# Third batch's first stage moved behind the second batch's last rows, two thirds of its stores put off, and the conditions at the end nested

## The chip, the cores and the metric

The kernel runs on one core of one Trainium2 chip. Its engines are TensorE (PE, matmuls), VectorE (DVE), ScalarE (ACT), GpSimd (POOL) and the queue engine SyncE (SP). ACT, POOL and SP also issue DMAs, each in the order of its own program. The metric is the device time of one execution in microseconds, the median of several runs.

## What is computed

```python
X = np.fft.rfft(x, axis=1)                     # x: (8, 2496, 256) float32
y = np.fft.irfft(X * F[None], n=2496, axis=1)  # F: one complex filter, 1249 x 256
...
x = y.reshape(8 * 2496, 256)                   # 19968 tokens
expert_idx = token_ids * 2654435761 % 8
out[mask_e] = np.maximum(x[mask_e] @ w1[e], 0) @ w2[e]     # w1[e]: 256 x 1024, w2[e]: 1024 x 256
```

A filter in the frequency domain is applied along each of 8 sequences (batches), and then each token goes through the one of 8 experts that its number picks.

## The kernel before, in words

**The filter.** The transform of length 2496 is split as 39 x 64. A batch (class `Batch`) passes three stages, all in float32.
- Stage 1 (`stage1(u)`, u = 0 to 5): matmuls `pa` (line 226, the last at 220) on rows of x, copied by ACT (line 228 or 223) into a tile `t1` on the chip. Each pair of u makes a part v = 0, 1, 2, which is stored to a table `d1` in DRAM at line 252: parts 0 and 1 have 960 KB, part 2 has 600 KB and 40 KB. ACT issues these stores for batch 2 and POOL for the later ones. `t1` has two places, which parts use in turn.
- Stage 2 (`stage2(u)`, u = 0 to 10): `load2(g)`, g = 0 to 4, brings two times 256 KB of `d1` back in another layout (line 258, on SP); `forward(u)` makes matmuls `pb` (line 267) and multiplies with the filter on DVE (lines 273 to 277); `back(u-1)` makes matmuls `pc` (line 289), copied by ACT. After every second one POOL stores two times 256 KB to a table `d2` (line 296).
- Stage 3 (`stage3(u)`, u = 0 to 5): `load4(v)` brings part v of `d2` back (`t<-d`, line 366, on SP), matmuls `pd` (line 226, the last at 220) make rows of tokens, ACT (batches 0 and 1) or DVE copies them to a tile `o`, and POOL writes each row of 117 tokens to its places in a DRAM table `xs`, sorted by expert, with an indirect DMA (`scatter`, line 385; four for each u, two for the last).

Batches 0 and 1 keep their middle tables on the chip; for them `turn4(u)` (matmuls `pu`, line 354) goes ahead of each `stage3(u)`.

**The experts.** `xs` is read in tiles of 128 tokens, of which 159 always exist and up to 163 may. `step(i)` handles tile i: `load(i + 4)` loads rows of a pair of tiles (`xg<-xs`, line 756, four loads of 64 KB), `numbers(i)` copies token numbers on POOL (line 773), `up(i)` makes 32 matmuls `ups` (line 790; relu at 794 on ACT and 796 on DVE), `down(i)` makes 16 matmuls `dps` (line 802), and POOL scatters the result to the output (line 806). `weights(i + 2, 0)` and `weights(i + 2, 1)` on SP load an expert's 1 MB of w1 (line 416) and of w2 (line 419) where the tile's expert differs. `turn(i + 1)` on DVE (line 780) prepares the next tile.

**The order.** It is written by hand. `todo` holds pairs of a time and a piece of work, sorted by time. Pieces with a time under 0 are emitted ahead of the tiles. For a time of 0 or more the whole part is the tile, and a fraction under .5 places the piece ahead of `up(i)`, one of .5 or more between `up(i)` and `down(i)` ("first slot" and "second slot" below). Times are no microseconds. Each engine works through its instructions in the order in which they were emitted; an instruction that waits holds up all behind it on its engine, DMA issues among them. `part1`, `part2` and `part3` list the times of a batch's stages 1, 2 and 3 and of their loads; `begin()` opens the tiles' buffers and issues `load(0)` to `load(3)`, half of them on ACT, the others on SP. The first tiles hold tokens of batches 0 and 1 alone, so `load(0)` waits for the last scatter of batch 1.

Before the change the pieces ahead of the tiles end as follows (t4 is `turn4`, s1 to s3 the stages, L1, L2 the loads of stages 1 and 2; batch, then index):

```
t4(1,0) s3(1,0) t4(1,1) s1(2,0) s3(1,1) t4(1,2) s1(2,1) s3(1,2) s1(2,2) t4(1,3) s1(2,3) s3(1,3) t4(1,4) s1(2,4) s3(1,4)
t4(1,5) s1(2,5) s3(1,5) L2(2,0) begin L2(2,1) L2(2,2) L2(2,3) L1(3,0) L1(3,1) s2(2,0)
```

**The end.** Tiles 159 to 162 stand in three blocks, each under its own condition `tc.If(used > first tile of the block)` at line 843, one after the other. With these inputs there are 159 tiles, and no block is entered.

Of the kernel before, what the change touches and what calls it, by code (L numbers as in the profile page):

```python
# [36 lines left out]
NU = (HN + XG) // XG  # L37
# [6 lines left out]
NT = (N + E * (TB - 1)) // TB  # L44
# [8 lines left out]
NSURE = NT - 4  # L53
# [66 lines left out]
def kernel(  # L120
# [10 lines left out]
    nc = tc.nc  # L131
# [45 lines left out]
    def slot(kind):  # L177
        slots[kind].append(slots[kind].pop(0))
        return slots[kind][-1]

    class Batch:


# [55 lines left out]
        def stage1(self, u):  # L239
            if self.d1 is None:  # L240
                self.d1 = dpool.tile([N2, 2 * NS, C], F32, name=f"d1_{self.b}", tag="d1")
            v, half = divmod(u, XL // XG)
            sl = slice(half * XG, half * XG + XG)
            if half == 0:
                self.t1 = slot("t1")
            self.products(wf_t, (NR, NR), 2 * NS, self.x[v][:, sl, :], self.t1[:, sl, :], nc.scalar.copy, u, "pa")
            if half == 1:


                eng = nc.scalar if self.b == 2 else nc.gpsimd  # L250
                for dram, chip in self.parts(self.d1, self.t1, v):
                    eng.dma_start(out=dram, in_=chip)

        def load2(self, g):
# [137 lines left out]
    batches = [Batch(b) for b in range(B)]  # L392
# [5 lines left out]
    def weights(i, which):  # L398

        if i >= NT:  # L400
            return
        if i >= 2 and which == 0:
            ws[i] = ws[i - 2][0:2]
        eng, kw = nc.sync, {}
        if which == 0:
            ws[i].append(eng.value_load(chunk_i[0:1, 0, i:i + 1], min_val=0, max_val=E - 1))
            if i >= 2:
                ws[i].append(eng.value_load(chunk_i[0:1, 1, i:i + 1], min_val=0, max_val=1))
        e = ws[i][2]
        if i >= 2:  # L410
            kw = {"cond": ws[i][3]}
        if which == 0:


            for f in (slice(0, F // 2), slice(F // 2, F)) if i < 2 else (slice(0, F),):
                eng.dma_start(out=ws[i][0][:, :, f],
                              in_=moe_w1[bass.ds(e, 1)].rearrange("one (p dp) f -> p (one dp) f", p=P)[:, :, f], **kw)
        else:
            eng.dma_start(out=ws[i][1], in_=moe_w2[bass.ds(e, 1)].rearrange("one (fp p) d -> p (one fp) d", p=P), **kw)
# [19 lines left out]
    def load_tables(part):  # L439
        if part < 2:  # L440

            nc.gpsimd.tensor_copy(junk[:], first.x[2 * part][0:1, 0, 0:1])
        sl = S_PARTS[part]
        nc.sync.dma_start(out=d_t[:, sl, :], in_=d_dram.ap()[:, sl, :])
        for k in range(2):
            load_filter(k, sl)
# [207 lines left out]
    def spaced(t0, t1, n):  # L654
        return [t0 + (t1 - t0) * u / n for u in range(n)]

    def part1(b, at, loads=None):
        bt = batches[b]
        if loads is None:

            loads = [at[2 * v] - 2.5 * (at[1] - at[0]) for v in range(NV)]
        return ([(at[u], lambda u=u: bt.stage1(u)) for u in range(NU)] +
                [(loads[v], lambda v=v: bt.load1(v)) for v in range(NV) if b > 0])

    def part2(b, at, ready):
        if isinstance(ready, list):
            bt = batches[b]
            return ([(at[u], lambda u=u: bt.stage2(u)) for u in range(NS // 2 + 1)] +
                    [(t, lambda g=g: bt.load2(g)) for g, t in enumerate(ready)])
        bt = batches[b]  # L670
        return ([(at[u], lambda u=u: bt.stage2(u)) for u in range(NS // 2 + 1)] +
                [(max(at[2 * g] - 4.5 * (at[1] - at[0]), ready), lambda g=g: bt.load2(g)) for g in range(NS // SG)])

    def part3(b, at, ready=None):
        bt = batches[b]
        if b < 2:
            return [(at[u], lambda u=u: bt.stage3(u)) for u in range(NU)]
        return ([(at[u], lambda u=u: bt.stage3(u)) for u in range(NU)] +
                [(max(at[2 * v] - 2.5 * (at[1] - at[0]), ready), lambda v=v: bt.load4(v)) for v in range(NV)])
# [4 lines left out]
    N_2 = NS // 2 + 1  # L684
# [8 lines left out]
    todo = [(t, lambda k=k: load_tables(k)) for k, t in enumerate((-160, -159, -157, -156))]  # L693
# [10 lines left out]
        todo += [(t - 2.6, lambda bt=bt, u=u: bt.turn4(u)) for u, t in enumerate(at)]  # L704
        todo += [(t, lambda bt=bt, u=u: bt.stage3(u)) for u, t in enumerate(at)]
    todo += [(-135, lambda: nc.sync.dma_start(out=wi_t[:], in_=wi_dram.ap()))]
    todo += part1(2, spaced(-102, -87, NU), [-119, -117.5, -116])
    todo += [(t, lambda k=k: weights(k // 2, k % 2)) for k, t in enumerate((-99, -98.9, -98.8, -98.7))]
    todo += [(-76, lambda: begin())]

    todo += part1(3, spaced(1.5, 6.5, NU), [-74.6, -74.5, 2.5]) + part1(4, spaced(15, 20.5, NU))
    todo += part1(5, spaced(21, 27, NU)) + part1(6, spaced(36, 46, NU)) + part1(7, spaced(50, 60, NU))
    todo += part2(2, [-74] + spaced(.55, 5.5, N_2 - 1), [-78, -75, -74.9, -74.8, 1.2]) + part2(3, spaced(9.2, 15.7, N_2), 6.6)
    todo += part2(4, spaced(22, 31, N_2), 20.5) + part2(5, spaced(31.2, 46, N_2), 28)
    todo += part2(6, spaced(48, 62, N_2), 47) + part2(7, spaced(63.2, 80, N_2), 61)
    todo += part3(2, spaced(7, 14, NU), 5.6) + part3(3, spaced(17, 25, NU), 15.6)
    todo += part3(4, spaced(33, 44, NU), 31.5) + part3(5, spaced(49, 63, NU), 46.5)
    todo += part3(6, spaced(67, 83, NU), 62) + part3(7, spaced(84, 101, NU), 81)
    todo.sort(key=lambda t: t[0])
# [46 lines left out]
    def numbers(i):  # L766

        if pair[i][0] != i:
            return
        g, n = xg[i][0], len(pair[i])  # L770
        no = nums.tile([P, 2], I32, name=f"no_{i}", tag="no")
        for a in range(4):
            nc.gpsimd.tensor_copy(no[32 * a:32 * a + 32, 0:n],  # L773
                                  g[96:128, a:4 * n:4, C // 4].bitcast(I32))
        for j in pair[i]:
            to_rows[j] = no[:, xg[j][1]:xg[j][1] + 1]

    def turn(i, to=None):
        xt[i] = work.tile([P, DP, TB], F32, name=f"xt_{i}", tag="xt")[:] if to is None else to
        nc.vector.transpose(out=xt[i].rearrange("p d (a t) -> p a d t", t=32),  # L780
                            in_=xg[i][0][:, 4 * xg[i][1]:4 * xg[i][1] + 4, 0:C // 4].rearrange("p a (c d) -> p a d c", d=DP))

    def up(i, ht):
        w1 = ws[i][0]
        for quad in range(FP // 4):
            ps = ups.tile([P, 4, TB], F32, name=f"ups_{i}_{quad}", tag="ups")
            for k in range(4):
                fp = 4 * quad + k
                for dp in range(DP):
                    nc.tensor.matmul(out=ps[:, k, :], lhsT=w1[:, dp, fp * P:(fp + 1) * P],  # L790
                                     rhs=xt[i][:, dp, :], start=(dp == 0), stop=(dp == DP - 1))
            dst = ht[:, 4 * quad:4 * quad + 4, :]
            if quad % 2 == 0:
                nc.scalar.activation(out=dst, in_=ps[:], func=AF.Relu)  # L794
            else:
                nc.vector.tensor_scalar_max(dst, ps[:], 0.0)  # L796

    def down(i, ht):
        w2 = ws[i][1]
        ps = dps.tile([P, 2, C], F32, name=f"dps_{i}", tag="d")  # L800
        for fp in range(FP):
            nc.tensor.matmul(out=ps[:, 0, :], lhsT=ht[:, fp, :], rhs=w2[:, fp, :],  # L802
                             start=(fp == 0), stop=(fp == FP - 1))
        o = outs.tile([P, C], F32, name=f"osb_{i}", tag="osb")
        nc.vector.tensor_copy(out=o[:], in_=ps[:, 0, :])  # L805
        st = nc.gpsimd.indirect_dma_start(  # L806
            out=out[:], out_offset=bass.IndirectOffsetOnAxis(ap=to_rows[i], axis=0),
            in_=o[:], in_offset=None, bounds_check=N - 1, oob_is_err=False)
        tc.declare_no_dep(st.ins, group="out_rows", reason="distinct rows")
        tc.add_to_no_dep_group("out_rows", st.ins)  # L810
# [4 lines left out]
    used = []  # L815
# [23 lines left out]
    spare = mid[:, 0, :].rearrange("p (i d t) -> p i d t", i=NT - NSURE, d=DP)  # L839
    for i in range(NSURE, NT):  # L840
        turn(i, spare[:, i - NSURE])
    for some in (range(NSURE, NSURE + 1), range(NSURE + 1, NSURE + 2), range(NSURE + 2, NT)):
        with tc.If(used[0] > some[0]):
            for i in some:
                ht = work.tile([P, FP, TB], F32, name=f"ht_{i}", tag="ht")
                numbers(i)
                up(i, ht)
                weights(i + 2, 0)
                down(i, ht)
                weights(i + 2, 1)  # L850


# [1 line left out]
_INS = ['x', 'filt_r', 'filt_i', 'moe_token_ids', 'moe_w1', 'moe_w2']  # L854
# [24 lines left out]
```

## Time and profile before

| what | value |
|---|---|
| time, median of 3 runs | 1522.52 us (1518.86 to 1523.35) |
| span of the profiled execution | 1528.2 us |
| mean granted TensorE clock | 0.982 |
| first `up` starts | 160.80 us |
| first `up` of tile 8 starts | 257.87 us |
| last matmul ends | 1514.1 us |
| DMA | 226.06 MB, mean 148 GB/s |

The profiled execution is one more run, and it is longer than the three timed ones. In the profile, a group `out<-in` is named after the program's tiles; `d` is a DRAM table (`d1` or `d2`), `mid` a tile in the stretch of memory that `t1`, the tables of stage 2 and their results share, `x` the input rows, `wts` the weights' buffers. A timeline line has start, duration, engine, source line, operation, tiles and shapes, number of instructions, and in brackets the idle time of the engine ahead of it and what is held to have ended it. SPq, ACTq and POOLq are the sequencers of those engines, which issue the DMAs.

The span has three parts: up to 142 us the filter of batches 0 and 1 with routing, without tiles; from 160.80 us to about 1085 us tiles with the filter of batches 2 to 7 between them; then tiles alone, 7.03 us from one `up` to the next.

### The profile page before, as it was taken

Reading aid. Unit: us, or ns where it says so; the run is one execution under the profiler, and the core shown is the slowest. Engines: PE = TensorE matmul, PEld = TensorE weight load, DVE = VectorE, ACT = ScalarE, POOL = GpSimd, SP = SyncE. Lnnn points to the kernel's source line nnn. Section 1 sums busy time; section 2 is a strip of 40 time slices with the busy share of each in tenths; the row PEclk is TensorE's granted clock in tenths of the full one; section 3 lists DMA queues with packets and bytes.
Section 4 is the critical chain, followed back from the end, with each engine's and each line's share of the span. In section 5 each row is a group of like instructions: output and inputs, shape, how many; then the busy total and the mean of one; then the engine's idle time right before and its main releaser. Section 6 shows DMA issues by size and latency. Waiting matters only on the chain.

```text
span 1528.2 us, 25837 instructions
## 1 busy us (share of the span) xinstructions
PE 1458.7 (95%) x9340; PEld 1338.2 (88%) x9340; DVE 539.1 (35%) x1008; ACT 233.8 (15%) x401; POOL 500.3 (33%) x802
## 2 busy tenths in 40 slices
PE   6996898999999999989999999999999999999996
PEld 6874787988989999979999999899999999999995
DVE  5962442642354443234434433222222122222221
ACT  3653120111121111111101010000000000000000
POOL 7465114544432343223331443233211211211111
PEclk9998899999999999999999999999999999999998
DMA  8256766559955863755657542643421423132320
GB/s 219 63 193 182 231 171 172 192 195 271 266 178 168 248 186 95 224 159 159 193 131 212 161 134 88 179 139 111 128 70 58 132 87 93 47 112 66 92 88 24
DMA packets 186989, 226.06 MB, mean 148 GB/s; under 512 B 101654, under 2 KB 157390, under 8 KB 180891
## 3 DMA queue, kind: packets, MB, share of 16 engines
q1 hardware_dynamic: 154615, 146.92, 35.1%
q0 software_dynamic: 28096, 73.51, 14.8%
q10 hardware_dynamic: 4147, 3.94, 0.9%
q8 instruction: 76, 1.25, 0.3%
q14 instruction: 55, 0.44, 0.1%
HBM read 415.94 MB, written 75.08 MB: 321 GB/s over the span
## 4 chain that ended last, share of the span: by engine, by line
PE 88%; DMA 7%; DVE 2%; issue 1%; POOL 1%; another core or an unknown queue 0%; SPq 0%; ACT 0%; ACTq 0%; POOLq 0%; DVEq 0%
PE ups L790 36%; PE dps L802 33%; PE pd L226 5%; PE pb L267 4%; PE pc L289 3%; PE pa L226 3%; DMA t<-d 1%; DMA wts<-in_moe_w_dram 1%; DMA wts<-in_x_dram 1%; PE pc L339 1%; PE pu L354 1%; DMA d_t<-d_tbl 1%; DMA mid<-d 1%; DMA x<-in_x_dram 1%; DVE z L276 1%
## 5 line engine op out<-in xcount | busy, mean ns | idle before, releaser
L790 PEld LDWEIGHTS ups<-xt,wts 128*128 128x128 f32 x5088 | 596.6, 193 | 15.9 <-issue 7.5
L790 PE MATMUL ups<-xt,wts 128*128 128x128 f32 x5088 | 598.0, 276 | 4.8 <-issue 3.3
L802 PE MATMUL dps<-wts,ht 128*128 128x256 f32 x2544 | 576.9, 379 | 4.3 <-DVE ht L796 2.4
L802 PEld LDWEIGHTS dps<-wts,ht 128*128 128x128 f32 x2544 | 474.2, 190 | 67.2 <-DVE ht L796 4.1
L806 POOL DMA_INDIRECT out_dram<-osb,no x159 | 158.4, 996 | 568.2 <-DVE osb L805 455.7
L796 DVE TENSOR_SCALAR ht<-ups 128x512 f32<-128x512 f32 x159 | 110.0, 692 | 503.2 <-PE ups L790 471.7
L794 ACT ACTIVATE ht<-ups 128x512 f32<-128x512 f32 x159 | 94.9, 597 | 875.0 <-PE ups L790 794.4
L385 POOL DMA_INDIRECT xs<-o,sidx x176 | 178.1, 1012 | 117.0 <-issue 48.5
L805 DVE COPY osb<-dps 128x256 f32<-128x256 f32 x159 | 67.6, 425 | 355.9 <-PE dps L802 335.4
L773 POOL COPY no<-xg 32x2 int32<-32x2 int32 (+1 forms) x328 | 60.5, 184 | 263.6 <-DMA out_dram<-osb,no 176.3
L276 DVE TENSOR_TENSOR z<-pb,filt 64x512 f32<-64x512 f32 x160 | 110.2, 689 | 2.3
L226 PE MATMUL pd<-t,wi_t 120*117 120x256 f32 x320 | 78.7, 389 | 6.6 <-DMA t<-d 6.6
L267 PE MATMUL pb<-mid,d_t 128*128 128x256 f32 x240 | 63.8, 389 | 16.1 <-DMA xg<-xs 12.5
L226 PEld LDWEIGHTS pd<-t,wi_t 120*117 120x117 f32 x320 | 58.1, 185 | 19.6 <-DMA t<-d 6.4
L273 DVE TENSOR_TENSOR y<-pb,filt 128x512 f32<-128x512 f32 x80 | 54.3, 679 | 58.6 <-PE pb L267 48.5
L292 ACT COPY mid<-pc 128x512 f32<-128x512 f32 x60 | 35.2, 586 | 229.3 <-PE pc L289 191.5
L780 DVE STREAM_TRANSPOSE xt<-xg 128x256 f32<-128x256 f32 x159 | 69.1, 435 | 0.0
L267 PEld LDWEIGHTS pb<-mid,d_t 128*128 128x128 f32 x240 | 44.3, 195 | 22.9 <-issue 13.7
L277 DVE TENSOR_TENSOR y<-y,z 128x512 f32<-128x512 f32 x80 | 61.5, 769 | 2.7
L289 PE MATMUL pc<-y,e_t 128*128 128x256 f32 x240 | 61.7, 379 | 0.0
L226 PE MATMUL pa<-x,wf_t 117*120 117x256 f32 x224 | 53.3, 380 | 1.0 <-issue 1.0
L289 PEld LDWEIGHTS pc<-y,e_t 128*128 128x128 f32 x240 | 45.4, 190 | 6.5 <-issue 0.4
(123 smaller groups left out, 554.8 us busy)
## 6 DMA issues: line engine op xcount, KB each, us to landing
wts<-in_moe_w_dram SPq DMA_DIRECT2D x320, 1024.0 KB
mid<-d SPq DMA_DIRECT2D x60, 256.0 KB
d<-mid POOLq DMA_DIRECT2D x60, 256.0 KB
xg<-xs SPq DMA_DIRECT2D x235, 64.0 KB
t<-d SPq DMA_DIRECT2D x12, 960.0 KB
x<-in_x_dram SPq DMA_DIRECT2D x36, 312.0 KB
d<-mid POOLq DMA_DIRECT2D x10, 960.0 KB
xg<-xs SPq DMA_DIRECT2D x77, 65.0 KB
```

What stands on the lines that cost most here:

```text
L226: nc.tensor.matmul(out=ps[0:cols * H, k, :], lhsT=w[:], rhs=src[:, 2 * i + k, :], start=True, stop=True)
L267: nc.tensor.matmul(out=ps[:, i, :], lhsT=d_t[:, s, :], rhs=rhs, start=True, stop=True)
L276: nc.vector.tensor_tensor(out=z[b], in0=ps[a], in1=f_t[1][a, sl, :], op=OP.mult)
L289: nc.tensor.matmul(out=ps[:, i, :], lhsT=e_t[:, 2 * u + i, :], rhs=pr[:, i, :], start=True, stop=True)
L385: st = nc.gpsimd.indirect_dma_start(out=xs[:], out_offset=bass.IndirectOffsetOnAxis(ap=index, axis=0), in_=rows, in_offset=None, bounds_ch ...
L780: nc.vector.transpose(out=xt[i].rearrange("p d (a t) -> p a d t", t=32), in_=xg[i][0][:, 4 * xg[i][1]:4 * xg[i][1] + 4, 0:C // 4].rearrang ...
L790: nc.tensor.matmul(out=ps[:, k, :], lhsT=w1[:, dp, fp * P:(fp + 1) * P], rhs=xt[i][:, dp, :], start=(dp == 0), stop=(dp == DP - 1))
L794: nc.scalar.activation(out=dst, in_=ps[:], func=AF.Relu)
L796: nc.vector.tensor_scalar_max(dst, ps[:], 0.0)
L802: nc.tensor.matmul(out=ps[:, 0, :], lhsT=ht[:, fp, :], rhs=w2[:, fp, :], start=(fp == 0), stop=(fp == FP - 1))
L805: nc.vector.tensor_copy(out=o[:], in_=ps[:, 0, :])
L806: st = nc.gpsimd.indirect_dma_start(out=out[:], out_offset=bass.IndirectOffsetOnAxis(ap=to_rows[i], axis=0), in_=o[:], in_offset=None, bou ...
```

## The change

- **Stage 1 of batch 2.** `s1(2,0)` and `s1(2,1)` keep their places; `s1(2,2)` to `s1(2,5)` are emitted behind `s3(1,5)`.
- **Its stores.** Part 0 is stored at once as before. The stores of parts 1 and 2 (960, 600 and 40 KB) are collected in `put_off` and issued by ACT behind `begin()`.
- **Stage 2 of batch 2.** `L2(2,0)` goes from ahead of `begin()` to behind those stores. `s2(2,0)` goes from ahead of the tiles to the second slot of tile 0; the others follow half a tile later than before, so that `s2(2,10)` is in the second slot of tile 5 instead of its first.
- **Stage 3 of batch 2.** `s3(2,0)` goes from tile 7 to tile 8, `s3(2,5)` from tile 12, second slot, to tile 13, first slot. `load4(2,0)` stays in tile 5, second slot; `load4(2,1)` goes from tile 6 to tile 7, `load4(2,2)` from tile 8 to tile 9.
- **Stage 1 of batch 6.** `s1(6,0)` goes from tile 36 to tile 35, `s1(6,5)` with the store of part 2 from tile 44, first slot, to tile 42, second slot.
- **The end.** The second condition stands inside the first one's block and the third inside the second's.

After the change the pieces ahead of the tiles end as follows:

```
t4(1,0) s3(1,0) t4(1,1) s1(2,0) s3(1,1) t4(1,2) s1(2,1) s3(1,2) t4(1,3) s3(1,3) t4(1,4) s3(1,4) t4(1,5) s3(1,5)
s1(2,2) s1(2,3) s1(2,4) s1(2,5) begin stores put off L2(2,0) L2(2,1) L2(2,2) L2(2,3) L1(3,0) L1(3,1)
```

```diff
@@ in stage1
-                for dram, chip in self.parts(self.d1, self.t1, v):
+                moves = self.parts(self.d1, self.t1, v)
+                if self.b == 2 and v > 0:
+                    put_off.extend(moves)
+                    return
+                for dram, chip in moves:
                     eng.dma_start(out=dram, in_=chip)
@@ the times
-    todo += part1(2, spaced(-102, -87, NU), [-119, -117.5, -116])
+    todo += [(t, lambda v=v: batches[2].load1(v)) for v, t in enumerate((-119, -117.5, -116))]
+    todo += [(t, lambda u=u: batches[2].stage1(u)) for u, t in enumerate((-101.5, -99.5, -86, -85.5, -85, -84.5))]
+    todo += [(-75.5, lambda: [nc.scalar.dma_start(out=dram, in_=chip) for dram, chip in put_off])]
...
-    todo += part1(5, spaced(21, 27, NU)) + part1(6, spaced(36, 46, NU)) + part1(7, spaced(50, 60, NU))
-    todo += part2(2, [-74] + spaced(.55, 5.5, N_2 - 1), [-78, -75, -74.9, -74.8, 1.2]) + part2(3, spaced(9.2, 15.7, N_2), 6.6)
+    todo += part1(5, spaced(21, 27, NU)) + part1(6, spaced(35, 44.5, NU)) + part1(7, spaced(50, 60, NU))
+    todo += part2(2, spaced(.55, 6, N_2), [-75, -74.9, -74.8, -74.7, 1.2]) + part2(3, spaced(9.2, 15.7, N_2), 6.6)
...
-    todo += part3(2, spaced(7, 14, NU), 5.6) + part3(3, spaced(17, 25, NU), 15.6)
+    todo += part3(2, spaced(8, 14.5, NU), 5.8) + part3(3, spaced(17, 25, NU), 15.6)
@@ the end
-    for some in (range(NSURE, NSURE + 1), range(NSURE + 1, NSURE + 2), range(NSURE + 2, NT)):
-        with tc.If(used[0] > some[0]):
-            for i in some:
+    blocks = [range(NSURE, NSURE + 1), range(NSURE + 1, NSURE + 2), range(NSURE + 2, NT)]
+    def rest(k):
+        with tc.If(used[0] > blocks[k][0]):
+            for i in blocks[k]:
...
+            if k + 1 < len(blocks):
+                rest(k + 1)
+    rest(0)
```

More of the change, by code (lines that the diff above doesn't have):

```diff
@@ L179, in slot @@
         return slots[kind][-1]
+    put_off = []
     class Batch:
```

## The prediction

> **What bounds the kernel now.** I read the page first.
>
> ```profile
> PE 1458.7 (95%) x9340; PEld 1338.2 (88%) x9340; DVE 539.1 (35%) x1008; ACT 233.8 (15%) x401; POOL 500.3 (33%) x802
> PE 88%; DMA 7%; DVE 2%; issue 1%; POOL 1%; another core or an unknown queue 0%; SPq 0%; ACT 0%; ACTq 0%; POOLq 0%; DVEq 0%
> ```
>
> TensorE is the bound; the change leaves its work as it is. So only stretches where PE stands still, or runs at half clock after standing still, can be won. PE's timeline shows where they are near the change:
>
> ```profile
> 140.91 2.03 PE L220 MATMUL pd<-t,wi_t 120*117 120x256 f32 x4 [3.02 <-issue]
> 155.44 2.04 PE L267 MATMUL pb<-mid,d_t 128*128 128x256 f32 x4 [12.51 <-DMA xg<-xs]
> 160.80 5.79 PE L790 MATMUL ups<-xt,wts 128*128 128x128 f32 x32 [3.32 <-issue]
> ...
> 244.48 3.76 PE L226 MATMUL pd<-t,wi_t 120*117 120x256 f32 x8 [6.03 <-DMA t<-d]
> 248.03 4.81 PE L790 MATMUL ups<-xt,wts 128*128 128x128 f32 x32
> ```
>
> Three waits: ahead of the tiles, 12.51 and 3.32 us; at tile 7, 6.03 us. Who feeds the first tile is in the timelines of POOL, ACT, SP and DVE:
>
> ```profile
> 141.75 0.99 POOL L385 DMA_INDIRECT xs<-o,sidx  x1 [0.30 <-DVE pads L610]
> 146.60 0.99 POOL L385 DMA_INDIRECT xs<-o,sidx  x1 [3.87 <-ACT o L223]
> 147.90 0.90 POOL L385 DMA_INDIRECT xs<-o,sidx  x1 [0.30 <-issue]
> 144.94 0.80 ACTq L252 DMA_DIRECT2D d<-mid  x2
> 150.72 1.82 ACTq L756 DMA_DIRECT2D xg<-xs  x4
> 149.75 1.44 SPq L258 DMA_DIRECT2D mid<-d  x2
> 151.57 3.06 SPq L756 DMA_DIRECT2D xg<-xs  x4
> 160.26 0.44 DVE L780 STREAM_TRANSPOSE xt<-xg 128x256 f32<-128x256 f32 x1
> ```
>
> Scatters follow each other every 1.30 us; the last two stood 3.57 us longer, for rows whose copies on ACT stood behind stage 1's. SP issued the first tile's rows behind load2, which had waited for the store of 144.94. DVE turned tile 0 only after `forward(0)`.
>
> The long chain names a third place, batch 6's first load2, issued at 646.55; PE stood 3.64 us for it.
>
> ```profile
> 646.55 6.72 DMA mid<-d
> 653.31 2.07 PE pb L267 x4
> ```
>
> The view of line 843 (the conditions), and of the program's last line, show the end:
>
> ```profile
> L843 POOLq INC_SWDGE_SEM  x3: 1742/1760/1781, 1514.7 to 1519.0; - x3
> L874 POOLq DRAIN  x3: 46/103/6607, 1520.8 to 1527.9; - x3
> ```
>
> PE has ended at 1514.1; POOL makes up the semaphores of three skipped blocks, one every 2.15 us, and then drains.
>
> **What the Trainium skill says.** "TensorE: Matmul & The Clock Gate", Part 1, has the array at half clock after about 3.4 us idle until it has been busy as long. The trace agrees: `ups` of a tile takes 3.57 us, but 5.79 at 160.80 and 4.81 at 248.03. "DMA: Bandwidth & Descriptors", "Issuing engines are not separate DMA queues", says that DMAs of ACT, SP and POOL share the same engines, so that a store moved to ACT's queue is not free beside other transfers. The trace agrees: a part of 960 KB stored from ACT at 125.73, beside a weight load, landed about 10.2 us later, while 640 KB at 144.94, nearly alone, took 4.7.
>
> **A, the start.** `s1(2,2)` to `s1(2,5)` are 4 x 1.73 us of PE less a bit for the last, with 8 ACT copies of 0.6. Behind `s3(1,5)` they still lie in the wait ahead of the tiles: cost nothing. The rows' last two scatters follow at once: 141.75 + 2 x 1.30 puts the last at 144.35, 3.55 earlier. It landed at 150.5, now at 147.0. ACT and SP issue the row loads at once, the last at 148.9; a set issued at 208.61 to 210.43 landed 1.8 us after its last issue, so 150.8, turn 0.44, and `up(0)` starts at 151.2 instead of 160.80.
>
> Behind it PE meets `s2(2,0)`, with `down(0)` and all other tiles queued behind. It needs stores put off (1600 KB), then load2. ACT issues the stores behind the rows, at 148.9. Price: 640 KB took 4.7 us; with about 2 us of that fixed (a 64 KB load's time), 240 KB/us, so 1600 KB take 8.7: landed 157.6. Bounds: at 94 KB/us, the congested rate above, 166; at 318 GB/s, the traffic in 130 to 140 us, 156. On SP, load2's two loads are issued in 1.0 us and land after 3.1 (those at 253.0): `pb` at 161.7. Behind them on SP wait the next load2s, batch 3's x loads and tile 4's rows; each has over 2 us to spare or is not needed before tile 3.
>
> PE: `up(0)` 151.2 to 157.0, idle 4.7, `pb` cold 2.0, `down(0)` 3.6 + 0.9 for half clock, `s2(2,1)` 1.7, `up(1)` 3.6, stage pieces 3.5, `down(1)` 3.4: 180.4. Before, the same `down(1)` ended at 183.8, with one unit of stage 2 (1.7) more done. **Gain 1.7 in this profile.**
>
> But the chain has 5.1 us at 139.46 under "an unknown queue", when ACT and DVE waited for matmuls already recorded as done. The timed runs are 5.7 us shorter than the span. If this stall belongs to the profiled execution alone, POOL's pace sets the rows in both kernels (landing 147.0), the old store goes at about 139, load2 lands by 147, and the kernel before starts `up(0)` at about 151.8 with `s2(2,0)` already done, 9.0 earlier than in the profile. Then A loses 9.0 - 1.7 = 7.3. I take the middle, **-2.8**, and keep both ends.
>
> **B, stage 3 of batch 2.** The wait at tile 7: 6.03, plus half clock (3.76 - 1.89 for `pd`, 4.81 - 3.73 for `ups`): 9.0. At 238.45 PE now goes on with tile 7, 7.03 us, and needs `t` at 245.5; it landed at 244.4, and `load4(2,1)`, which ran beside it, is issued about 4 us later. `s2(2,10)` half a tile later delays d2's store only to about 227.4, while POOL came to it at 230.89, behind `numbers(5)`. **Gain 9.0** (3 to 9). All later load4s keep over 20 us.
>
> **C, batch 6.** Its last d1 store (640 KB) leaves the stretch 620 to 640 us, in which DMA is 92 to 98% busy. At about 300 GB/s (284 to 352 in the windows up to 635) that is 2.1 us of transfer ahead of batch 7's x loads, for whose landing SP stood ahead of load2. 3.64 shrinks to about 1.5, and half clock (1.0 + 0.4) mostly goes. **Gain 3.0** (0 to 5.1).
>
> **D, the end.** If nested blocks are made up for in one go, two of three rounds go: 2 x 2.15. If every semaphore keeps its own instruction of 1.76, only the branches between go, 0.7. No row shows nesting; nothing suggests a loss. I take **4.2**.
>
> Everything else (the order of pieces within tiles 0 to 13) only changes places in a full PE: nothing, since DVE's load there is about 8.5 of 10 to 12 us a tile.
>
> **The sum.** Against its own span: 1.7 + 9.0 + 3.0 + 4.2 = 17.9, 1510.3 from 1528.2. Against the timed runs, with A at -2.8: 13.4, so 1522.5 - 13.4 = **1509.1**. 0.3%, 4.6 us, is about what can be told from no change here.
>
> **The rivals.**
> - *The wait moves on to tile 8* (17%). For: SP and POOL have much queued there, and `t` took 10.4 us. Against: 1.1 us in hand and a load less beside it. B falls to 3: 1515.1.
> - *The nesting doesn't merge anything* (15%): D is 0.7, 1512.6.
> - *Slower: the stores put off hold up the tiles* (8%). PE, first tile, `pb` of `s2(2,0)`. The slowest load of a part in view, `t<-d` at 235.06, took 14.1 us for 960 KB beside others, 68 KB/us; 1600 KB would take 23.5, landing 172.4, `pb` at 176.5, 14.8 later than I put it: 1523.9. It decides from `pb` at 175.1 on. For: row loads in pieces of 256 B run at the same time. Against: no weight load and few scatters run then.
>
> **Chances.** The forecast has 60%. Range: best case, A +1.7, B 9, C 5.1, D 4.3, is 1502.4, and the runs before spread by 4.5, so 1501; the low side takes in a middle rate of the stores (166 for the landing, 8.4 more: 1517.5) and the first two rivals: 1519. Faster by over 0.3%: 82%; within: 12%; slower: 6%.
>
> **What would show it.** A: `up(0)` near 151, then PE idle 4 to 5 us ahead of `pb` of line 267; scatters 1.30 apart to the end. B: no wait on `t<-d` near tile 8. C: under 2 us ahead of `pb` in tile 48. D: one INC_SWDGE_SEM and an end about 4 us nearer the last matmul. I am wrong if `pb` comes after 170, if `t` still makes PE wait, or if POOL still counts three rounds.

## The result, and the profile after

| kernel | median, us | runs |
|---|---|---|
| before | 1522.39 | 4 (1518.86 to 1523.35) |
| after | 1509.71 | 4 (1508.77 to 1509.82) |

The ratio is 0.992, with a 95% interval of 0.9902 to 0.9937: 12.2 us faster, 9.6 to 14.9. The forecast was 1509.1. The total came out. Of its four parts, B and D make the gain, C gave nothing that can be told, and what A costs stays open.

The profiled execution of after has a span of 1507.1 us. The page's first part:

```profile
PE 1454.8 (97%) x9340; PEld 1338.0 (89%) x9340; DVE 538.4 (36%) x1008; ACT 234.6 (16%) x401; POOL 495.2 (33%) x802
```

PE's busy time has hardly moved (1458.7 before), its share has grown from 95 to 97%. PE's timeline of after, at the places that the prediction named:

```profile
145.36 6.46 PE L799 MATMUL ups<-xt,wts 128*128 128x128 f32 x32 [10.11 <-DVE xt L789]
...
156.62 2.04 PE L273 MATMUL pb<-mid,d_t 128*128 128x256 f32 x4 [4.80 <-DMA mid<-d]
158.46 4.95 PE L811 MATMUL dps<-wts,ht 128*128 128x256 f32 x16
...
238.68 1.89 PE L228 MATMUL pd<-t,wi_t 120*117 120x256 f32 x8
...
338.47 3.57 PE L228 MATMUL pd<-t,wi_t 120*117 120x256 f32 x8 [4.10 <-DMA t<-d]
...
639.06 2.07 PE L273 MATMUL pb<-mid,d_t 128*128 128x256 f32 x4 [2.22 <-DMA mid<-d]
```

(Lines 799, 273, 811 and 228 of after are 790, 267, 802 and 226 of before.) The reader is to see five things, from the top. `up(0)` starts at 145.36, and nothing of batch 2 stands ahead of it. PE then stops for 4.80 us ahead of `pb`, where the forecast had 4.7. `pd` of batch 2's stage 3 at 238.68 has no bracket: the wait of 6.03 is gone. In tile 17 there is a wait of 4.10 for batch 3's `t`, where the first profile of before has 0.60. Ahead of batch 6's `pb` there are 2.22 us, not 3.64.

The feeders of the first tile, in the timelines of POOL, ACT and SP:

```profile
138.70 0.90 POOL L391 DMA_INDIRECT xs<-o,sidx  x1 [0.30 <-issue]
141.03 2.33 ACTq L765 DMA_DIRECT2D xg<-xs  x4
144.06 2.93 ACTq L716 DMA_DIRECT2D d<-mid  x3
152.81 4.97 SPq L264 DMA_DIRECT2D mid<-d  x8
```

The last row is scattered at 138.70, ACT's half of the row loads follows, then the three stores put off, and SP starts load2 8.75 us after the first of them was issued.

The end, in the views of line 854 (the conditions) and line 888 (the program's last):

```profile
L854 POOLq INC_SWDGE_SEM  x1: 1802/1802/1802, 1497.8 to 1497.8; - x1
L888 POOLq DRAIN  x3: 46/103/6607, 1499.6 to 1506.8; - x3
```

One round of semaphores is left of three. The last of the drains takes 6.6 us as before.

The two spans differ by 21.1 us, the medians of the timed runs by 12.7. The profiled execution of before was a long one, as the next section shows.

### The profile page after: what moved, and what is told of

Read it like the earlier page. It is cut to its first block, busy times and chain, and to the rows that moved or that the text cites. A ratio compares the mean times of both kernels' runs of the same rounds, so it can differ in the third digit from the quotient of the medians.

```text
span 1507.1 us, 25818 instructions
## 1 busy us (share of the span) xinstructions
PE 1454.8 (97%) x9340; PEld 1338.0 (89%) x9340; DVE 538.4 (36%) x1008; ACT 234.6 (16%) x401; POOL 495.2 (33%) x802
## 4 chain that ended last, share of the span: by engine, by line
PE 90%; DMA 5%; DVE 2%; issue 1%; POOL 1%; SPq 0%; ACT 0%; ACTq 0%; POOLq 0%; DVEq 0%
PE ups L799 36%; PE dps L811 35%; PE pd L228 5%; PE pb L273 4%; PE pc L295 3%; PE pa L228 3%; DMA wts<-in_x_dram 1%; PE pc L345 1%; DMA wts<-in_moe_w_dram 1%; DMA t<-d 1%; DMA d_t<-d_tbl 1%; DMA d<-mid 1%; DMA mid<-d 1%; PE pu L360 1%; DVE z L282 1%
## 5 line engine op out<-in xcount | busy, mean ns | idle before, releaser
L391 POOL DMA_INDIRECT xs<-o,sidx x176 | 176.6, 1003 | 98.2 <-issue 44.3
L273 PEld LDWEIGHTS pb<-mid,d_t 128*128 128x128 f32 x240 | 44.3, 195 | 13.0 <-issue 5.4
```

The source lines that it names most:

```text
L273: nc.tensor.matmul(out=ps[:, i, :], lhsT=d_t[:, s, :], rhs=rhs, start=True, stop=True)
L391: st = nc.gpsimd.indirect_dma_start(out=xs[:], out_offset=bass.IndirectOffsetOnAxis(ap=index, axis=0), in_=rows, in_offset=None, bounds_ch ...
```

## The experiments

The kernels ran in three groups, each on one chip (1, 2, 3 in the table) and timed against the kernel before on that chip.

| kernel | chip | median, us | before, us | ratio to before | 95% interval |
|---|---|---|---|---|---|
| before again | 1 | 1521.96 (one run) | 1520.32 | | |
| D alone | 1 | 1516.86 | 1520.32 | 0.9985 | 0.9974 to 0.9995 |
| B alone | 1 | 1511.88 | 1520.32 | 0.9960 | 0.9945 to 0.9974 |
| A alone | 1 | 1519.85 | 1520.32 | 0.9997 | 0.9985 to 1.0009 |
| after again | 2 | 1521.44 | 1528.50 | 0.9949 | 0.9929 to 0.9968 |
| after without A | 2 | 1515.47 | 1528.50 | 0.9921 | 0.9894 to 0.9947 |
| C alone | 2 | 1528.74 | 1528.50 | 1.0002 | 0.9987 to 1.0018 |
| after, blank rows later | 2 | 1518.83 | 1528.50 | 0.9937 | 0.9916 to 0.9958 |
| after, stage 2 of batch 2 later | 3 | 1519.52 | 1521.01 | 0.9987 | 0.9978 to 0.9995 |
| after, stores at once | 3 | 1508.77 | 1521.01 | 0.9913 | 0.9896 to 0.9930 |
| after, both (stage 2, blank rows) | 3 | 1512.58 | 1521.01 | 0.9936 | 0.9920 to 0.9953 |
| after without A, blank rows later | 3 | 1500.14 | 1521.01 | 0.9860 | 0.9839 to 0.9881 |

Runs of one kernel spread by 5 us and more. In the profiles of the next table up to 3.6 us of it is there by 110 us, in work that no part of the change touches. So I also compare profiles by stretches, which leave the start out. "To tile 6" and "to tile 14" count from the `pu` that follows a wait of 0.78 us, at 106 to 110 us, to `up(6)` and `up(14)`; the other columns are from `up` of one tile to `up` of another, and from `up(158)` to the end.

| kernel (chips 1 and 3, and the first profile of after) | to tile 6 | to tile 14 | 14 to 18 | 18 to 49 | 158 to end |
|---|---|---|---|---|---|
| before again | 114.3 | 203.7 | 48.0 | 300.6 | 21.35 |
| D alone | 115.4 | 203.2 | 47.5 | 300.0 | 17.44 |
| A alone | 117.3 | 203.8 | 48.0 | 299.7 | 21.34 |
| B alone | 113.7 | 194.4 | 47.0 | 299.9 | 21.35 |
| after (A, B, C, D) | 116.7 | 197.4 | 47.1 | 299.7 | 17.45 |
| after, stores at once | 116.8 | 197.5 | 47.6 | 301.5 | 17.45 |
| after without A, blank rows later | 117.8 | 198.6 | 41.1 | 298.6 | 17.45 |

**The kernel before, profiled again.** No edit.

> The kernel before, profiled once more. Theory 1 (the stall at 139.46 us belongs to the one execution that was profiled): the span is about 1521, the last two scatters are issued about 144 to 145 and up(0) starts at about 152, after s2(2,0) is done. Theory 2 (the stall is the kernel's own): span 1527 to 1529, up(0) at about 160.8.

PE's timeline in it:

```profile
148.25 2.04 PE L267 MATMUL pb<-mid,d_t 128*128 128x256 f32 x4 [13.66 <-DMA mid<-d]
153.62 5.41 PE L790 MATMUL ups<-xt,wts 128*128 128x128 f32 x32 [3.32 <-issue]
...
236.49 3.76 PE L226 MATMUL pd<-t,wi_t 120*117 120x256 f32 x8 [5.61 <-DMA t<-d]
...
346.19 3.74 PE L226 MATMUL pd<-t,wi_t 120*117 120x256 f32 x8 [4.07 <-DMA t<-d]
```

The span is 1520.2 and `up(0)` comes at 153.62: theory 1, though the last scatter was issued at 140.51 already. The reader is to see the last line too: the wait in tile 17, which looks new in after, is in the kernel before as well (4.07). The first profile of before showed little of it; there, tiles 14 to 18 took 44.0 us, not 48.0. So the change has not moved a wait to tile 17; it has left one there. The stall isn't one execution's either. On chip 2 three of four profiles have one, of 5.2 to 7.6 us. After's second profile has it in its chain of waits:

```profile
129.13 5.16 another core or an unknown queue
```

On that chip all kernels are slower, before by 8 us, and from tile 49 to 158 PE needed 840.6 to 841.9 us, against 837.0 to 839.2 on the others; the first profile of before has 840.6. It looks like a profile of such a chip beside times of another, which the record doesn't say. What PE does in the stall stays open.

**D alone.** The three blocks nested, as in the change; all else as before.

> The kernel before with the nested conditions alone. Forecast (one round of semaphore making-up instead of three): 3.9 to 4.3 us shorter, one INC_SWDGE_SEM in the profile. Rival (nesting saves only the branches): 0.7 us shorter, three INC_SWDGE_SEM.

The view of its line of conditions:

```profile
L845 POOLq INC_SWDGE_SEM  x1: 1798/1798/1798, 1502.7 to 1502.7; - x1
```

One round. From `up(158)` to the end every kernel of the table with nested conditions needs 17.44 or 17.45, every other 21.34 or 21.35: 3.9 us. The timed gain of 0.8 to 4.0 us agrees; the rival's 0.7 is just outside it, and the rival expected three rounds.

**B alone.**

```diff
-    todo += part3(2, spaced(7, 14, NU), 5.6) + part3(3, spaced(17, 25, NU), 15.6)
+    todo += part3(2, spaced(8, 14.5, NU), 5.8) + part3(3, spaced(17, 25, NU), 15.6)
```

> The kernel before with stage 3 of batch 2 later alone. Forecast: the 6.03 us wait at tile 7 and its half clock go, 9 us shorter. Rival, from the changed kernel's profile, where PE waits 4.10 us for t<-d of batch 3 in tile 17 (0.60 before): part of the gain is given back there, so only 5 to 6 us shorter, with the gap ahead of pd in tile 17 or 18 about 3.5 us longer than before.

PE's timeline:

```profile
236.38 1.89 PE L226 MATMUL pd<-t,wi_t 120*117 120x256 f32 x8
...
336.07 3.54 PE L226 MATMUL pd<-t,wi_t 120*117 120x256 f32 x8 [4.00 <-DMA t<-d]
```

No wait at tile 8, and the one in tile 17 is as long as in before. To tile 14 the stretch is 9.0 us shorter (203.4, the mean of before and D alone, less 194.4), and from there on nothing is given back: the rival, that part goes back in tile 17, has read a wait as new that was old. Timed, B is worth 4.0 to 8.4 us by the interval, 8.4 by the medians: the 9.0 of the profiles lies a little above.

**A alone.** Stage 1 of batch 2 moved, its stores put off, its stage 2 half a tile later; stage 3, batch 6 and the end as before.

> The kernel before with stage 1 of batch 2 moved, its stores put off and the first unit of stage 2 moved alone. Forecast (the old stall is not usual, so A loses): 2.8 us longer, up to 7.3. Rival (the old stall is usual): 1.7 us or more shorter. From the changed kernel's profile, by its sum against the timed runs: about 0, within 2 us. In all cases the wait ahead of pb in tile 0 is 4 to 5 us; stage 3 of batch 2 waits in tile 7 or 8 as before (5 to 7 us), since its load is bound by d2's store and not by PE, so what A wins or loses ahead of it may vanish there.

```profile
238.26 2.83 PE L228 MATMUL pd<-t,wi_t 120*117 120x256 f32 x8 [3.80 <-DMA t<-d]
```

Nothing in time (0.9997) and nothing to tile 14 (203.8 against 203.4). As expected, the wait at tile 7 takes up what A does ahead of it: it is 3.80 here and 5.61 in before again. A loss is hidden as long as that wait stands. Where B is in, it can show: 197.4 with A (after), 194.4 without (B alone), 3.0 us lost.

That is one pair, and the start of a kernel without A varies. `up(6)` lies ahead of the wait at tile 7, so there all seven kernels of the table compare: 116.7 to 117.3 with A, but 113.7 to 117.8 without. One piece of it is the same in all: from `up(2)` to `up(6)` the three with A take 45.7 us and the four without 44.0. With A, PE makes one more unit of stage 2 there (four `pb` and four `pc` matmuls more); without A it makes this unit ahead of the tiles, where it stands idle for the most part. So 1.7 us of A's price is shown. At `up(2)` a kernel with A is between 2.9 us ahead and 1.9 behind, depending on the profile that it is compared with.

**After again, and after without A.** The second has stage 1 of batch 2, its stores and `s2(2,0)` as in the kernel before, with B, C and D.

> The changed kernel once more, as a measure beside the three that follow. Expected: 1508 to 1512 and the same gaps as in its first profile (4.8 ahead of pb in tile 0, about 4 ahead of pd in tile 17, 2.2 ahead of pb in tile 48).

> The changed kernel with part A undone (stage 1 of batch 2, its stores and the first unit of stage 2 as before; B, C and D kept). Counted from the pu of line 354 or 360 at about 107 to 108 us, which ends a wait in every profile, the changed kernel starts tile 14 3.0 us later than the kernel with B alone. Theory (A loses about 3, as the forecast's -2.8 had it): this kernel is 3 us faster than the changed one, about 1506.5, and starts tile 14 195 us after that pu instead of 198. Rival (A wins 1.7 or more): it is slower than the changed one, 1511 or more. Rival 2 (A wins nothing, loses nothing, because a later wait takes up the slack): within 1 us.

On this chip both have the stall, and after's gaps are not those of its first profile: in tile 0 it stands 6.69 us ahead of `pb`, in tile 17 only 0.87. Without A it is 1515.47 against 1521.44, 6.0 faster, in the direction of the first theory. But the intervals of the two ratios overlap, and the stall's length differs between profiles of the same work: to tile 14, after again and the kernel with blank rows later are alike, and their profiles differ by 5.1 us there (209.8 and 204.7). That A loses is likely; how much, 0 to 6 us, isn't settled.

**C alone.**

```diff
-    todo += part1(5, spaced(21, 27, NU)) + part1(6, spaced(36, 46, NU)) + part1(7, spaced(50, 60, NU))
+    todo += part1(5, spaced(21, 27, NU)) + part1(6, spaced(35, 44.5, NU)) + part1(7, spaced(50, 60, NU))
```

> The kernel before with stage 1 of batch 6 earlier alone. Forecast: the wait ahead of pb in tile 48 (3.27 in the second profile of before, 3.64 in the first) falls to about 1.5 and the kernel is 3.0 us shorter. Rival (from the profiles: the wait is 2.22 in the changed kernel, 2.77 with B alone and 2.72 with D alone, both without C): C is worth 0 to 1 us, the wait stays between 2.2 and 3.3.

```profile
657.12 1.13 PE L267 MATMUL pb<-mid,d_t 128*128 128x256 f32 x4 [3.03 <-DMA mid<-d]
```

The wait is 3.03 and the time the same: the rival. SP in this kernel, and (second fence) in before again:

```profile
648.49 1.78 SPq L756 DMA_DIRECT2D xg<-xs  x4
650.44 6.68 SPq L258 DMA_DIRECT2D mid<-d  x6
```

```profile
638.57 1.85 SPq L756 DMA_DIRECT2D xg<-xs  x4
640.53 7.37 SPq L258 DMA_DIRECT2D mid<-d  x6
```

SP issues load2 right behind the rows of a tile in both. So what sets its start seems to be its place in SP's queue, and the store that C moves is issued by POOL and isn't in that queue. The unit's two loads had landed 6.6 us after the first issue here and 8.1 in before again; but PE needed them 3.6 us after it here and 4.8 in before again. Over all profiles the wait is 2.3 to 3.6 us in the five without C and 1.7 to 3.3 in the nine with it. No run moves load2 itself, so that an earlier place would win these 3 us isn't shown.

**After, blank rows later.** The last stage's tiles have places without a token, for which `pads()` scatters blank rows, 7 DMAs on POOL.

```diff
-    ... (-80, blanks), (14.6, pads)]
+    ... (-80, blanks), (26.6, pads)]
```

> The changed kernel with the scatters of blank rows (7 on POOL, 1.28 us apart, slot 14.6) put at slot 26.6. Theory (the 4.1 us wait for t<-d of batch 3 in tile 17 comes from d2's last store standing behind those scatters on POOL's queue): that store is issued 3 to 6 us earlier against PE, the wait falls under 1 us, its half clock goes too (3.57 - 1.89), and the kernel is 4 to 6 us faster than the changed one. Rival (the load is slow by itself, 11.5 us beside tile rows and x loads): the wait stays above 3.

POOL in after, with the last of those scatters ahead (321.21, another 0.97 us), and then POOL and PE in this kernel:

```profile
322.49 0.97 POOL L815 DMA_INDIRECT out_dram<-osb,no  x1 [0.30 <-issue]
323.45 1.14 POOL L302 DMA_DIRECT2D d<-mid  x2
```

```profile
327.07 1.01 POOL L815 DMA_INDIRECT out_dram<-osb,no  x1 [6.98 <-DVE osb L814]
329.89 1.14 POOL L302 DMA_DIRECT2D d<-mid  x2 [1.82 <-ACT mid L298]
...
346.26 1.89 PE L228 MATMUL pd<-t,wi_t 120*117 120x256 f32 x8
```

In after, the store to `d2` (line 302) is issued 10.9 us ahead of the moment at which PE needs `t` (334.37); here it is 16.4 ahead, released by ACT's copy and not by POOL's queue, and `pd` has no wait. Tiles 14 to 18 take 41.07 us in all three kernels with the blank rows later, on two chips, against 47.1 in after: 6.0 us, 4.1 of wait and 1.7 of half clock in `pd`. (3.57 for `pd` in place of 1.89, at a granted clock of 0.53 from 338.4 to 342.0 us, is what the Trainium skill, "TensorE: Matmul & The Clock Gate", Part 1, says of an array that has stood idle for over 3.4 us.) On chip 2, where after again needs 44.3 us from tile 14 to 18, the timed gain over it is 2.6 us by the medians, less than the intervals can tell.

**After, stage 2 of batch 2 later.**

```diff
-    todo += part2(2, spaced(.55, 6, N_2), ...
+    todo += part2(2, spaced(1.1, 6.1, N_2), ...
```

> The changed kernel with stage 2 of batch 2 spread from slot 1.1 to 6.1 instead of 0.55 to 6, so that its first unit stands behind down(0) and no longer ahead of it. Theory (A's loss is the 4.8 us that PE stands ahead of pb in tile 0 and the half clock behind it, since the rows themselves come 7 us earlier): the wait falls to 1 us or less, and the kernel is 4 to 6 us faster than the changed one. Rival (the put-off stores land too late in any case): pb waits 3 us or more behind down(0), and the time stays within 2 us of the changed kernel's.

In this kernel load2(2,4), at 1.2, fills the buffer of load2(2,0) ahead of unit 1 at 1.55, so unit 1 of batch 2's stage 2 is made from other rows than the reference's; number and sizes of the instructions are the same. PE's timeline:

```profile
160.99 1.10 PE L273 MATMUL pb<-mid,d_t 128*128 128x256 f32 x4 [1.73 <-DMA mid<-d]
...
171.94 3.56 PE L228 MATMUL pa<-x,wf_t 117*120 117x256 f32 x8 [6.28 <-DMA x<-in_x_dram]
180.88 2.05 PE L273 MATMUL pb<-mid,d_t 128*128 128x256 f32 x4 [5.38 <-DMA mid<-d]
```

The 4.80 fell to 1.73. But then PE, with less work ahead, came to batch 3's stage 1 before its x had landed (6.28). In after these x loads, which stand behind load2 on SP, landed at 167.3 and 168.7, just as PE came (168.55). The 5.38 behind is this kernel's own: unit 1 waits for the load that took the buffer. (That is read from the order of the pieces.) So the time of this kernel (0.9987) is no price of the idea, and the experiment decides neither of its theories; what it does show is that x of batch 3 is needed next.

**After, stores at once.**

```diff
-                if self.b == 2 and v > 0:
+                if self.b == 2 and v > 9:
```

> The changed kernel with no store put off: ACT issues the stores of parts 1 and 2 of batch 2 behind their copies, so ahead of the row loads of tile 0. Theory (putting them off is what makes pb wait): the stores land some 6 us earlier, the wait of 4.8 ahead of pb in tile 0 falls under 1.5, up(0) starts no more than 1 us later, and the kernel is 4 to 5 us faster than the changed one. Rival (the forecast's price for stores beside other traffic): the last scatters and the row loads land later by 3 us or more, up(0) with them, and nothing is won.

PE's timeline, then, of the last ten scatters (the view of `xs` on POOL from 128 us), the line on landing, here and (last fence) in after:

```profile
153.90 6.26 PE L799 MATMUL ups<-xt,wts 128*128 128x128 f32 x32 [17.65 <-DVE xt L789]
```

```profile
DMA to landing us min/median/max: 3.7/7.8/8.7
```

```profile
DMA to landing us min/median/max: 2.7/2.8/4.9
```

Each theory has half of it. The wait ahead of `pb` is gone, as the first has it; but scatters took 7.8 us to land and not 2.8, and `up(0)` starts 7.6 us later (45.0 against 37.4 after the `pu`). That is what the Trainium skill, "DMA: Bandwidth & Descriptors", "Issuing engines are not separate DMA queues", says: ACT's stores and POOL's scatters share engines. At tile 14 the two kernels are level to 0.1 us (197.5 and 197.4), and in time as well (0.9913 and 0.992). Putting the stores off moved the wait from ahead of `up(0)` to behind it, and won nothing.

**Both of the first two, and after without A with the blank rows later.**

> The changed kernel with stage 2 of batch 2 at 1.1 to 6.1 and the scatters of blank rows at slot 26.6, both. If the two waits are apart in time and nothing else takes them up: 7 to 11 us faster than the changed kernel (4 to 6 in tile 0, 3 to 6 in tile 17), about 0.986 of the kernel before. If a later wait takes up the first gain: 3 to 6 us.

> The kernel before with B, C and D and the scatters of blank rows at slot 26.6, A undone. Theory (A as it stands loses 3 to 6, the pads' place 3 to 6): 6 to 11 us faster than the changed kernel, about 0.987 of the kernel before. It is the measure for A with its first unit of stage 2 moved: if that kernel is faster than this one, A's idea wins once nothing waits for the stores.

The first has the same changed unit as the kernel with stage 2 later, and its waits of 6.91 and 5.25 in tile 1; it does not gain on after. But it differs from stage 2 later in the place of the blank rows alone, on the same chip, and is 6.9 us faster (0.9936 against 0.9987, the intervals apart): that is the timed measure of their place. The second, PE's timeline:

```profile
157.89 5.22 PE L790 MATMUL ups<-xt,wts 128*128 128x128 f32 x32 [3.31 <-issue]
...
337.36 1.89 PE L226 MATMUL pd<-t,wi_t 120*117 120x256 f32 x8
```

It is the fastest of all: 0.986, 0.9839 to 0.9881, whose interval lies wholly below that of after (0.9902 to 0.9937): 1500.14 us. Its tile 17 has no wait. Of the 9.6 us to after's median (on another chip) the 6.0 in tile 17 are accounted for. Its start was no better than after's in its one profile (198.6 to tile 14 against 197.4); in B alone, with the same start, it was better (194.4). With stage 1 as before the last scatters land beside batch 2's stores, and how long these hold them up differs: PE stood 17.30 us ahead of `pb` here and 13.66 in before again. So what A costs beyond the unit of stage 2 stays open here as well.

## Why the prediction was right, point by point

- **The sum.** 13.4 us were forecast, 12.2 measured (9.6 to 14.9). Against the second group's chip, the same kernel gained 7.8 (0.9949; 4.9 to 10.9). That 1509.1 and 1509.7 lie so close is in part luck: C, put at 3.0, gave nothing, the four parts timed alone add up to 8.5 us by their ratios, and an interval of 5 us can't test terms of 3.
- **The long profile of before.** The forecast set a span against timed runs and found 5.7 us. A timed run is 1.7 us longer than its span (1508.77 and 1507.1 of one execution of after), so the profiled execution was 7.4 us longer than the timed ones. Its span is 8.0 over that of before again: 7.0 more from that `pu` to `up(14)`, where the stall lies, 4.0 less from tile 14 to 18, 3.4 more from 49 to 158, and 1.6 elsewhere.
- **A, -2.8.** Likely right in sign, and near the 3.0 of one pair of profiles, but that is luck: 2.8 was the middle of two readings, one drawn from the long profile and one with a loss of 7.3. Its steps in after: the scatters ran 1.30 apart to the end. The wait ahead of `pb` was 4.80 (4.7). The stores landed 8.6 us after their first issue, at 152.7 (8.7 at 240 KB/us). `up(0)` came at 145.36 and not at 151.2, which had been reckoned from the long profile. The forecast's second reading, that the stall is not in most executions and that `up(0)` of before comes at about 151.8 with `s2(2,0)` done, was right (153.62). Its loss of 7.3 was too large: it put `up(0)` of after 0.6 us ahead of that of before, and counted from the `pu` it is 6.8 ahead of before again (37.4 and 44.2). POOL's pace is the same in both, as it said (the last scatter at 30.8 and 31.1); but in before again load2 landed for `pb` at 148.25, not by 147, and `up(0)` stands behind `pb`.
- **B, 9.0.** 9.0 between profiles, 4.0 to 8.4 timed. The margin at tile 8 was 1.1 us in the forecast and 2.7 in the trace (`t` landed at 236.0, `pd` at 238.68). The rival "the wait moves on to tile 8" is refuted, and so is its kin at tile 17, by the second profile of before. But "all later load4s keep over 20 us" doesn't hold for batch 3's: PE stood 0.60 us for it in the forecast's own profile and 4.0 to 4.6 in seven others.
- **C, 3.0.** This is the term that failed: measured alone 1.0002, from 2.0 us faster to 2.8 slower. The step was "3.64 shrinks to about 1.5", from 2.1 us of transfer leaving the stretch. The store did leave, but load2 started no earlier against PE, behind a tile's rows in SP's order, and from its first issue to `pb` it took 6.5 to 7.6 us in the profiles with C and 7.2 to 8.1 in those without. The wait was 3.03 with C alone and 2.22 in after, where the profiles without C have 2.28 to 3.64.
- **D, 4.2.** 3.9 in the profiles, 0.8 to 4.0 timed, from one round in place of three. The rival (0.7, three rounds) is refuted.
- **The slower rival**, stores that hold up the tiles to `pb` at 175.1: `pb` came at 156.62. Refuted; with stores at once it is the scatters that they hold up, not the tiles behind.

## What to carry to other kernels

In a stretch that transfers feed, moving one of them moves the wait: compare the kernels at a point behind the whole stretch, not at the wait that went. For each wait on a load, walk back through the queues that issue the load and its store, and look for work there with no haste of its own; here, 7 scatters of blank rows on POOL cost some 6 us. And profile the kernel before twice: a wait may be hidden in one profile and seem new in the next.

## What the runs showed of the hardware

- POOL makes up the semaphores of nested blocks in one instruction of 1.80 us, where three blocks side by side took three of 1.76.
- The same kernel took 1520.3, 1521.0 and 1528.5 us on three chips. On the slowest, three of four profiles have 5.2 to 7.6 us in their chains, between 122 and 148 us, put down to "another core or an unknown queue", with no cause on record.
- Ten scatters of rows landed in a median of 2.8 us in after, where the DMA engines were busy 38% of the time from 128 to 141 us, and in 7.8 us, at 75%, beside two stores of 960 and 640 KB issued from another engine.
- `pd` took 3.57 us at a granted clock of 0.53 after a wait of 4.10 us, and 1.89 us in tile 17 without a wait.
